# Pooled attention and a gated MLP on one core: 23 of 35 output DMAs move from SyncE's queue to ScalarE's

## The chip, the cores and the metric

The kernel runs on one core of a Trainium2 chip. The metric is the time of one execution on the device in microseconds (us), taken as the median of repeated runs. The core has five engines that run side by side, each with an instruction stream of its own: TensorE (PE in the profile; PEld is its weight loads), VectorE (DVE), ScalarE (ACT), GpSimd (POOL) and SyncE (SP). In this kernel SP computes nothing; it issues DMAs, one after the other. ACT computes and can issue DMAs too. An engine's stream is strictly in order: an instruction that waits holds all that stand behind it on that engine.

## The reference, cut to what matters

```python
# q, k, v: (8, 8, 576, 64), pooled attention
k_p = k.reshape(B, H, Sp, 8, D).mean(axis=3)
v_p = v.reshape(B, H, Sp, 8, D).mean(axis=3)
attn = softmax(q @ k_p.T / sqrt(D))
x = (attn @ v_p).transpose(0, 2, 1, 3).reshape(4608, 512)
# w1, w2: (512, 1024), w3: (1024, 1024), w_out: (1024, 512)
h = ((x @ w1) * (x @ w2)) @ w3
out = h @ w_out                      # (4608, 512) float32
```

## The kernel before, in words

The 4608 tokens are worked on in twelve chunks of 384 (`m` or `n`, 0 to 11); a chunk has three output tiles of 128 tokens (`t`, 0 to 2). fp32 matrices are kept as a high and a low part, and a product is made of three matmul passes (`PASSES`, line 771). At the start `w3 @ w_out` is multiplied once into `W` (`w_mm`, line 1046), so that a chunk needs `a = x @ w1`, `b = x @ w2`, the product `g = a * b`, and `g @ W`.

For chunks 0 to 7 the steps are `a_mm` and `b_mm` (the matmuls of line 783), `a_post` (ACT copies `a` out of PSUM, line 793), `b_post` (DVE multiplies, line 803), `g_hi` (ACT, line 808), `g_lo` (DVE, line 813) and `out_mm` (line 831), eight times (`j`). Chunks 8 to 11 go in two pairs (`M` = 4, 5) with seven products of blocks in place of eight (`prod`, line 960). The blocks of their weights were mixed earlier and written to DRAM (`ws`); SP loads them into a ring of 11 slots, some steps ahead (`load_u`, line 945), each load waiting until PE has read the slot's former block. `s1_copy`, `s5_copy` and `s2_copy` (ACT, lines 966, 971, 974) take the products out of PSUM.

Attention of chunk n+1 runs between these: `s_mm` (line 531), softmax on DVE and ACT (lines 547 to 592), a transposition by way of DRAM: `te_turn` (DVE, lines 656, 657), `te_out` (SP writes `D<-T` and `D<-Tr`, lines 665, 666), `te_in` (SP reads back `PTl<-D` and `PTr<-D`, four DMAs each, lines 687, 691), `te_post` and `te_rest` (ACT, lines 701 and 696; DVE, 703 and 697), then `av_mm` (line 735).

When the matmuls of a chunk's output are done, `out_post` (line 851) copies each of the three PSUM banks to an SBUF tile `ob` (pool `osp`, three buffers, shared with the tiles of the weight mixing) and sends it to DRAM. ACT copies tiles 0 and 2 (line 863), DVE tile 1 (line 861). Chunk 11's tile 2 is split in halves (lines 853 to 858) whose DMAs go out on ACT and SP already (line 857).

The order of each engine's stream is fixed by a hand-made plan of due times (`plan`, `SHIFT`, `LATER`); the change touches none of it. The framework counts the landing of DMAs on eight counters (DMAHW0 to DMAHW7), which the program's DMAs use in turn, whichever engine issues them. A DMA is issued only when the one that used its counter before has landed. So a DMA on one queue can wait for one of the other queue.

Of the kernel before, what the change touches and what calls it, by code (L numbers as in the profile page):

```python
# [19 lines left out]
def kernel(  # L20
# [14 lines left out]
    nc = tc.nc  # L35
# [3 lines left out]
    P = 128  # L39
# [70 lines left out]
        out=msk,  # L110
        in_=ident.rearrange("p (q j e) -> p j q e", j=4, e=KR),
# [707 lines left out]
    def out_t(m, j, t):  # L819
        if j == 0 and t == 0:  # L820
            oacc[m] = [pacc.tile([P, 512], F32, tag=f"o{t}", name=f"o{t}") for t in range(3)]
            if m == NCH - 1:
                oacc["end"] = oacc[m][2], patt.tile([P, 512], F32, tag="att", name="att")
        g, gh, gl = gt[m, j]
        c = slice(t * P, (t + 1) * P)
        parts = [(oacc[m][t], slice(0, DM))]
        if m == NCH - 1 and t == 2:
            parts = [(oacc["end"][i][:, :HD], slice(i * HD, (i + 1) * HD)) for i in range(2)]
        for o, d in parts:
            for i, (sg, sw) in enumerate(PASSES):  # L830
                nc.tensor.matmul(out=o, lhsT=(gh, gl)[sg][:, c], rhs=W[j][sw][:, d],  # L831
                                 start=(j == 0 and i == 0), stop=(j == NJ - 1 and i == 2))
        if t == 2:
            gt.pop((m, j))
        if m == NCH - 1 and j == NJ - 1:
            out_post(m, t)
# [14 lines left out]
    def out_post(m, t):  # L851
        r0 = m * CH + t * P
        if m == NCH - 1 and t == 2:
            for i, copy in enumerate((nc.scalar.copy, nc.vector.tensor_copy)):
                half = p2.tile([P, HD], F32, tag="a", name="a")
                copy(out=half, in_=oacc["end"][i][:, :HD])
                (nc.scalar, nc.sync)[i].dma_start(out=out[r0:r0 + P, i * HD:(i + 1) * HD], in_=half)
            return
        ob = osp.tile([P, DM], F32, tag="ob", name="ob")
        if t == 1:  # L860
            nc.vector.tensor_copy(out=ob, in_=oacc[m][t])  # L861
        else:
            nc.scalar.copy(out=ob, in_=oacc[m][t])
        nc.sync.dma_start(out=out[r0:r0 + P], in_=ob)

    B11, B21, B22, T1, T2, T3, T4 = range(NU)
    HALVES = (0, 2)
# [493 lines left out]
    for m in range(NP):  # L1361
        m0 = M0 + 3 * NJ * m
        for j in range(NJ):
            k = m0 + 3 * j
            at("M", k, a_mm, m, j)
            at("P", k + 1, a_post, m, j)
            at("M", k + 1, b_mm, m, j)
            at("P", k + 2, b_post, m, j)
            at("P", k + 2, g_hi, m, j)
            at("P", k + 2.5, g_lo, m, j)  # L1370
            at("M", k + 5 + 1.2 * ((m, j) == (NP - 1, NJ - 1)), out_mm, m, j)
        for t in range(3):
            at("P", m0 + 3 * NJ + 3 + 2 * (m == NP - 1), out_post, m, t)
# [16 lines left out]
    for M in range(NP // 2, NCH // 2):  # L1390
        m0 = M0 + 6 * NJ * M
        for j in range(NJ):
            k = m0 + STEP * j
            for i, x in enumerate((0, 0.68, 1.24, 1.92, 2.48, 3.16, 4.45)):
                at("M", k + x, prod, M, j, i)
                units.append((int(k + x), M, j, i))
            for fn, x in STEADY.items():
                if fn in (g_hi, g_lo):
                    at("P", k + x, fn, 2 * M, j)
                else:  # L1400
                    at("P", k + x, fn, M, j)
            if j < NJ - 1:
                for x, lo, hi in ((6.8, 0, 1), (8.03, 1, 2), (8.71, 2, 8), (10.56, 8, 9)):
                    at("M", k + x, out_some, 2 * M, j, lo, hi)
            else:
                at("M", k + 5.2, out_some, 2 * M, j, 0, 9)
        k = m0 + STEP * NJ
        for t in range(3):
            at("P", k + 1, out_post, 2 * M, t)
        for j in range(NJ):  # L1410
            at("P", k + j, g1_hi, M, j)
            at("P", k + j, g_lo, 2 * M + 1, j)
            at("M", k + 1 + j + 3.2 * (j == NJ - 1 and M < NCH // 2 - 1), out_mm, 2 * M + 1, j)
        if M < NCH // 2 - 1:
            for t in range(3):
                at("P", k + 5 + NJ, out_post, 2 * M + 1, t)
# [72 lines left out]
```

## Time and profile before

| what | us |
|---|---|
| median of 3 runs | 744.12 (744.02 to 744.53) |
| the profiled execution, its own time | 740.84 |
| span of its instructions | 739.1 |
| PE busy | 731.1 (99%) |
| DVE busy | 461.3 (62%) |
| ACT busy | 351.8 (48%) |
| POOL busy | 175.4 (24%) |

The profile is of one execution. Its own time is 1.7 us above its span and 3.3 us below the median of the runs. Busy is the time in which an engine executes; DMA issues and waits are not counted in it. PE's granted clock is 0.999 of full speed over the span. The first chunk's outputs are copied at 142 us, the last chunk's at 734 us.

### The profile page before, as it was taken

To read this page: it belongs to the slowest core of one execution; us is meant where nothing else is said; L and a number is where in the kernel's file an instruction comes from. 1 tells how busy PE (TensorE), PEld (TensorE's weight loads), DVE (VectorE), ACT (ScalarE), POOL (GpSimd) and SP (SyncE) were. 2 spreads that over 40 slices of the span, in tenths; PEclk is the share of its full clock that TensorE was granted. 3 is DMA by queue.
4 is the path that set the end of the run, shared out by engine and by line. 5 is a ranking of instruction groups with operands and counts; after the bars stand their busy time and mean duration, and the time that the engine had idled before them with its cause. 6 is when DMAs were issued, how large, how long until landed. Compare 5 with 4: busy or idle time off the path is not lost.

```text
span 739.1 us, 12234 instructions
## 1 busy us (share of the span) xinstructions
PE 731.1 (99%) x4088; PEld 682.5 (92%) x4088; DVE 461.3 (62%) x913; ACT 351.8 (48%) x1059; POOL 175.4 (24%) x228
## 2 busy tenths in 40 slices
PE   8999999999999999999999999999999999999997
PEld 7888999999999999999999999999999999899996
DVE  5788877655675835664657658465886586633342
ACT  7888986442442644434433435353454344422222
POOL 2245384033431531004503313044042000000000
PEclk9999999999999999999999999999999999999999
DMA  9979934187386465486656462736498859176611
GB/s 327 344 241 298 330 120 122 55 229 184 109 210 156 145 163 151 128 193 189 176 130 186 130 171 81 148 127 154 96 333 266 226 170 314 41 236 199 197 57 44
DMA packets 177743, 132.62 MB, mean 179 GB/s; under 512 B 78352, under 2 KB 145104, under 8 KB 177680
## 3 DMA queue, kind: packets, MB, share of 16 engines
q1 hardware_dynamic: 177536, 131.70, 62.6%
q8 instruction: 33, 0.54, 0.3%
q14 instruction: 30, 0.25, 0.1%
q10 hardware_dynamic: 144, 0.13, 0.1%
HBM read 94.63 MB, written 37.16 MB: 178 GB/s over the span
## 4 chain that ended last, share of the span: by engine, by line
PE 95%; DMA 2%; DVE 1%; SPq 1%; issue 0%; ACT 0%; ACTq 0%
PE o L831 22%; PE a L783 18%; PE b L783 18%; PE a L960 8%; PE att L531 5%; PE att L735 5%; PE o L1052 4%; PE o L846 4%; PE att L960 4%; PE b L960 2%; DMA raw<-in_moe_w_dram 1%; PE b L1052 1%; PE a L1052 1%; DMA D<-T 1%; PE att L238 1%; DMA PTl<-D 0%
## 5 line engine op out<-in xcount | busy, mean ns | idle before, releaser
L831 PE MATMUL o<-Wc,gh 128*128 128x512 f32 (+1 forms) x480 | 149.2, 392 | 0.0
L783 PE MATMUL b<-xT,hl 128*128 128x384 f32 x768 | 145.7, 339 | 0.0
L783 PE MATMUL a<-xT,hl 128*128 128x384 f32 x768 | 145.6, 338 | 0.0
L783 PEld LDWEIGHTS a<-xT,hl 128*128 128x128 f32 x768 | 133.4, 188 | 2.9
L783 PEld LDWEIGHTS b<-xT,hl 128*128 128x128 f32 x768 | 132.8, 188 | 0.0
L808 ACT CAST gh<-a 128x384 fp32r<-128x384 f32 x80 | 41.1, 514 | 126.8 <-DVE a L803 101.7
L831 PEld LDWEIGHTS o<-Wc,gh 128*128 128x128 f32 x480 | 87.5, 188 | 13.8 <-DVE ob L861 0.2
L831 PE MATMUL o<-Wc,gl 128*128 128x512 f32 (+1 forms) x240 | 93.1, 388 | 0.0
L569 ACT ACTIVATE E<-att,mx 128x72 f32<-128x72 f32 (+1 forms) x240 | 73.3, 323 | 28.3 <-DVE mx L547 26.5
L960 PE MATMUL a<-X,ring 128*128 128x384 f32 x384 | 77.4, 337 | 0.9 <-ACT tmp L974 0.6
L960 PEld LDWEIGHTS a<-X,ring 128*128 128x128 f32 x384 | 67.8, 188 | 4.4 <-ACT tmp L974 1.0
L803 DVE TENSOR_TENSOR a<-b,a 128x384 f32<-128x384 f32 x64 | 35.2, 550 | 55.5 <-PE b L783 53.8
L468 POOL TENSOR_TENSOR st<-st 128x512 f32<-128x512 f32 (+2 forms) x29 | 39.8, 1371 | 114.0 <-DMA st<-in_v_dram 65.2
L793 ACT COPY a<-a 128x384 f32<-128x384 f32 x64 | 30.7, 480 | 75.2 <-PE a L783 75.0
L831 PEld LDWEIGHTS o<-Wc,gl 128*128 128x128 f32 x240 | 45.1, 188 | 10.2 <-DVE gl L813 0.7
L813 DVE TENSOR_TENSOR gl<-a,gh 128x384 fp32r<-128x384 f32 x80 | 47.1, 589 | 7.0 <-ACT gh L808 6.6
L880 POOL TENSOR_TENSOR mix<-mix 128x256 f32<-128x256 f32 x16 | 11.9, 744 | 162.1 <-DMA mix<-wr 118.8
L569 ACT ACTIVATION_READ_ACCUMULATOR E<-att,mx 128x1 f32 (+1 forms) x240 | 50.0, 208 | 0.0
L531 PE MATMUL att<-kbd,qT 128*128 128x144 f32 (+1 forms) x320 | 49.9, 286 | 0.0
L531 PEld LDWEIGHTS att<-kbd,qT 128*128 128x128 f32 (+1 forms) x320 | 45.8, 179 | 1.7
L547 DVE TENSOR_REDUCE mx<-att 128x4 f32<-128x288 f32 (+1 forms) x80 | 35.3, 446 | 15.3 <-PE att L531 14.9
L960 PE MATMUL att<-X,ring 128*128 128x384 f32 x192 | 38.8, 338 | 0.0
(160 smaller groups left out, 1161.9 us busy)
## 6 DMA issues: line engine op xcount, KB each, us to landing
ring<-ws SPq DMA_DIRECT2D x112, 256.0 KB
raw<-in_moe_w_dram SPq DMA_DIRECT2D x32, 512.0 KB
out_dram<-ob SPq DMA_DIRECT2D x35, 256.0 KB
st<-in_v_dram SPq DMA_DIRECT2D x16, 512.0 KB
ws<-mix SPq DMA_DIRECT2D x32, 256.0 KB
st<-in_k_dram SPq DMA_DIRECT2D x24, 288.0 KB
qs<-in_q_dram SPq DMA_DIRECT2D x112, 48.0 KB
D<-T SPq DMA_DIRECT2D x7, 768.0 KB
```

The costliest lines, as they stand in the source:

```text
L468: eng.tensor_tensor(out=t[:, :, 0:4], in0=t[:, :, 0:4], in1=t[:, :, 4:8], op=ALU.add)
L531: nc.tensor.matmul(out=ps[:nt, 2 * KP * j:2 * KP * (j + 1)], lhsT=qT[n][:, pr, off:off + nt], rhs=kbd[b % 2][:, pr], start=True, stop=True,)
L547: nc.vector.tensor_reduce(out=mx[:nt, hs], in_=sv, axis=AX.X, op=ALU.min)
L569: nc.scalar.activation(out=E[:nt, h], in_=sv[:, i], func=AF.Exp, scale=-1.0, bias=mx[:nt, h:h + 1], accum_out=sm[:nt, h:h + 1])
L735: nc.tensor.matmul(out=Tp[n, pr, "x"][:, off:off + cnt], lhsT=parts[x][0], rhs=parts[x][1], start=x == 0, stop=x == 3)
L783: nc.tensor.matmul(out=o, lhsT=w12[j, w][sw][:, kt * P:(kt + 1) * P], rhs=x[sx][:, kt], start=(i == 0), stop=(i == 3 * NK - 1))
L803: nc.vector.tensor_tensor(out=g, in0=ps[:, :CH], in1=g, op=ALU.mult)
L808: nc.scalar.copy(out=gh, in_=g)
L813: eng.tensor_tensor(out=gl, in0=g, in1=f(gh), op=ALU.subtract)
L831: nc.tensor.matmul(out=o, lhsT=(gh, gl)[sg][:, c], rhs=W[j][sw][:, d], start=(j == 0 and i == 0), stop=(j == NJ - 1 and i == 2))
L960: nc.tensor.matmul(out=o, lhsT=w[:, kt, sw], rhs=x[sx][:, kt], start=first and n == 0, stop=n == 5, skip_group_check=True)
L1052: nc.tensor.matmul(out=wacc[h][it], lhsT=w3t[s][sa][:, it * P:(it + 1) * P], rhs=wo[j][sb], start=(j == 0 and i == 0), stop=(j == NJ - 1 a ...
```

## The change

In `out_post` the DMA of a tile that DVE copied (`t == 1`) stays with SP, and the DMA of a tile that ACT copied (tiles 0 and 2 of chunks 0 to 10, tile 0 of chunk 11: 23 of them) is put in ACT's own stream, right behind the copy.

```diff
             nc.vector.tensor_copy(out=ob, in_=oacc[m][t])
         else:
             nc.scalar.copy(out=ob, in_=oacc[m][t])
-        nc.sync.dma_start(out=out[r0:r0 + P], in_=ob)
+        (nc.sync if t == 1 else nc.scalar).dma_start(out=out[r0:r0 + P], in_=ob)
```

The streams of PE, DVE and POOL are the same as before. Three places show what moves. `waits` names the counters that an instruction waits for: those of DMA landings, and those of the engines.

ACT at the outputs of chunk 7 (`ob_6272` and `ob_6278` are tiles 0 and 2), before:

```order
L569 ACTIVATE E_6190,sm_6192<-att_6179,mx_6191 96x72 x3
L863 COPY ob_6272<-o0_5599 128x512 [waits PE_49]
L863 COPY ob_6278<-o2_5601 128x512 [waits PE_49]
L966 COPY a_6305<-a_6296 128x384 [waits PE_49,Activation_49]
L569 ACTIVATE E_6282,sm_6284<-att_6267,mx_6283 96x72 [waits DVE_49,Activation_49]
```

and now:

```order
L863 COPY ob_6272<-o0_5599 128x512 [waits PE_49]
L864 DMA out_0_dram<-ob_6272 128x512 [waits DMAHW7_49,Activation_49]
L863 COPY ob_6278<-o2_5601 128x512 [waits PE_49]
L864 DMA out_0_dram<-ob_6278 128x512 [waits DMAHW2_49,Activation_49]
L966 COPY a_6305<-a_6296 128x384 [waits PE_49]
```

Each DMA waits for ACT's own copy and for a landing, and stands ahead of the next copy and of line 966.

SP at the same place, before:

```order
L945 DMA ring_6270<-ws_102 128x512 [waits DMAHW0_49,PE_49]
L864 DMA out_0_dram<-ob_6272 128x512 [waits DMAHW1_49,Activation_49]
L864 DMA out_0_dram<-ob_6275 128x512 [waits DMAHW2_49,DVE_49]
L864 DMA out_0_dram<-ob_6278 128x512 [waits DMAHW3_49,Activation_49]
L945 DMA ring_6303<-ws_102 128x512 [waits DMAHW4_49,PE_49]
L945 DMA ring_6331<-ws_102 128x512 [waits DMAHW5_49,PE_49]
L945 DMA ring_6333<-ws_102 128x512 [waits DMAHW6_49,PE_49]
L665 DMA D_6335<-T_6251 96x1024 [waits DMAHW7_49,DVE_49]
```

and now:

```order
L864 DMA out_0_dram<-ob_6275 128x512 [waits DMAHW3_49,DVE_49]
L945 DMA ring_6303<-ws_102 128x512 [waits DMAHW4_49,PE_49]
L945 DMA ring_6331<-ws_102 128x512 [waits DMAHW5_49,PE_49]
L945 DMA ring_6333<-ws_102 128x512 [waits DMAHW6_49,PE_49]
L665 DMA D_6335<-T_6251 96x1024 [waits DMAHW7_49,DVE_49]
```

SP has one output there in place of three and waits for DVE's copy alone. The transposition's write of line 665 now shares counter 7 with ACT's output `ob_6272`.

SP at the outputs of chunk 5, the four `PTr` reads (line 691) of the transposition, before:

```order
L691 DMA PTr_4706<-D_4842 32x3x128 [waits DMAHW5_49]
L691 DMA PTr_4706<-D_4842 32x3x128 [waits DMAHW6_49]
L691 DMA PTr_4706<-D_4842 32x3x128 [waits DMAHW7_49]
L691 DMA PTr_4706<-D_4842 32x3x128 [waits DMAHW0_49]
L358 DMA qs_4859<-in_q_dram 32x12x32 [waits DMAHW1_49]
```

and now:

```order
L691 DMA PTr_4706<-D_4842 32x3x128 [waits DMAHW7_49]
L691 DMA PTr_4706<-D_4842 32x3x128 [waits DMAHW0_49]
L691 DMA PTr_4706<-D_4842 32x3x128 [waits DMAHW1_49]
L691 DMA PTr_4706<-D_4842 32x3x128 [waits DMAHW2_49]
L358 DMA qs_4859<-in_q_dram 32x12x32 [waits DMAHW3_49]
```

The counters of ACT's two outputs of chunk 5 are 7 and 1: the first of the four reads now waits until tile 0 has landed, the third until tile 2 has.

## Rows read from the trace of the kernel before

**Rows 1.** The page's part 1: busy time, share of the span, instructions.

```profile
PE 731.1 (99%) x4088; PEld 682.5 (92%) x4088; DVE 461.3 (62%) x913; ACT 351.8 (48%) x1059; POOL 175.4 (24%) x228
```

**Rows 2.** Waits of PE's matmuls: who waited for whom, total us, times, longest.

```profile
...
PE a L960 <- ACT tmp L974: 0.6, 1, 0.6
PE a L960 <- DVE tmp L985: 0.3, 1, 0.3
```

**Rows 3.** Waits of SP's queue, the longest row.

```profile
SPq L864 <- ACT ob L863: 66.5, 9, 22.2
```

**Rows 4.** DMA issues by line: times, ns min/median/max, first and last start.

```profile
L864 SPq DMA_DIRECT2D out_dram<-ob x35: 332/371/565, 143.5 to 735.3; - x35
L945 SPq DMA_DIRECT2D ring<-ws x112: 319/326/1767, 521.2 to 700.6; - x112
```

**Rows 5.** Timeline of chunk 11's outputs: start, us, engine, line, what.

```profile
734.51 1.13 SPq L864 DMA_DIRECT2D out_dram<-ob  x2
735.30 0.42 DVE L856 COPY a<-att 128x256 f32<-128x256 f32 x1
735.35 0.37 ACTq L857 DMA_DIRECT2D out_dram<-a  x1
735.75 0.38 SPq L857 DMA_DIRECT2D out_dram<-a  x1
```

**Rows 6.** Timeline of chunk 7's outputs, on DVE, ACT, SP, PEld.

```profile
546.82 0.65 DVE L861 COPY ob<-o 128x512 f32<-128x512 f32 x1
...
547.85 1.07 ACT L863 COPY ob<-o 128x512 f32<-128x512 f32 x2
...
548.46 1.31 SPq L864 DMA_DIRECT2D out_dram<-ob  x3
...
549.86 1.50 SPq L945 DMA_DIRECT2D ring<-ws  x3
550.01 0.48 ACT L966 COPY a<-a 128x384 f32<-128x384 f32 x1 [1.09 <-PE a L960]
...
552.10 1.00 PEld L960 LDWEIGHTS att<-X,ring 128*128 128x128 f32 x6 [0.20 <-ACT tmp L971]
```

**Rows 7.** Timeline of chunk 2's outputs: ACT behind them, and PE.

```profile
259.59 0.48 ACT L793 COPY a<-a 128x384 f32<-128x384 f32 x1
...
262.69 1.03 PE L783 MATMUL a<-xT,hl 128*128 128x384 f32 x5
```

**Rows 8.** Timeline behind chunk 10's last output: ACT, DVE, PEld.

```profile
718.67 0.52 ACT L999 CAST gh<-g 128x384 fp32r<-128x384 f32 x1
...
719.22 0.56 DVE L813 TENSOR_TENSOR gl<-g,gh 128x384 fp32r<-128x384 f32 x1 [0.64 <-ACT gh L999]
...
720.64 0.19 PEld L831 LDWEIGHTS o<-Wc,gl 128*128 128x128 f32 x1
```

**Rows 9.** Timeline of chunk 5's outputs, on ACT, SP, PE.

```profile
425.94 0.59 ACT L863 COPY ob<-o 128x512 f32<-128x512 f32 x1 [0.39 <-PE o L831]
426.47 1.84 SPq L691 DMA_DIRECT2D PTr<-D  x4
...
431.93 0.82 ACT L696 CAST PTr<-PTr 64x768 fp32r<-64x768 f32 x1
...
434.35 0.27 PE L735 MATMUL att<-PTr,VR 128*128 128x192 f32 x1
```

**Rows 10.** SP's timeline of chunk 0's outputs; line 874 reuses tile 0's buffer.

```profile
143.55 1.33 SPq L864 DMA_DIRECT2D out_dram<-ob  x3
...
145.65 0.63 SPq L874 DMA_DIRECT2D mix<-wr  x1
```

**Rows 11.** The chain of work that ended last, behind chunk 7's outputs.

```profile
560.55 1.05 PE att L960 x6
562.48 5.38 DMA D<-T
...
569.19 3.52 DMA PTl<-D
```

## The prediction

> **What bounds the kernel now.** I read the page first, then PE's waits, then SP's, then the timelines around the places where outputs leave. PE is busy for 731.1 of a span of 739.1 us [rows 1], so all of its idle time is 8.0 us. Of that some 3.8 lie behind its last matmul: DVE's last copy starts at 735.30, right behind PE's end, and the span ends at 739.1 [rows 5]. PE's waits have six rows: four belong to the weights' preparation (lines 236 to 264), ahead of any output, and the two that are shown come later, of 0.6 and 0.3 us, both around the start of the block products [rows 2]. So between the first output and the last matmul there is 0.9 us that a better order of transfers could give back, and the reader should see from this that a large gain is not there to be had, however long SP's waits are. SP does wait long for the copies that ACT makes: 66.5 us in nine waits, the longest of 22.2 [rows 3]. None of it shows up on PE: what SP loads is loaded early.
>
> **The change, part by part.** *On ACT, 23 issues are added.* ACT's one issue in this trace, for chunk 11's half tile, took 0.37 us [rows 5], and SP's 35 issues of outputs 0.33 to 0.57, median 0.37 [rows 4]. The issue also breaks the overlap of neighbouring copies (two of 0.59 take 1.07 together, so 0.1 is lost) and needs a gap of about 0.1 to the next instruction (three of SP's issues take 1.31, against 1.11 for three medians) [rows 4, 6]. That makes 0.57 us of ACT's stream for each output, 13 us in all, on an engine that is busy for 352 of 739 us [rows 1]. Whether it costs time is decided at each of the twelve places:
>
> - Chunks 0, 2, 6: the two copies run back to back, so what follows on ACT comes 2 x 0.57 = 1.14 us later. Chunk 2 is the tightest: line 793's copy of `a` moves from 259.59 to 260.73 and ends at 261.21, and PE writes that bank again at 262.69 [rows 7]. Slack 1.5 us, cost nothing. Were both issues as slow as SP's slowest of all, 1.77 [rows 4], 2.8 more would be asked and 1.3 lost.
> - Chunk 7: the copies start at 547.85; 1.07 + 1.14 later it is 550.06, and line 966, which waits for PE, started at 550.01 [rows 6]. So 0.05 us late. Here nothing is spare: two copies later PE's weight load already waits 0.20 us for ACT [rows 6], so a delay goes through to PE one to one. With issues of 0.33 it is nothing, with 0.57 it is 0.45. I take 0.05, since the median is what ACT's own issue showed.
> - Chunks 1, 3, 4, 5, 8, 9, 10, 11: the second copy waits for PE anyhow, and ACT idles behind it. Chunk 10 is the tightest: line 999's cast moves from 718.67 to 719.24, line 813 from 719.22 to 719.79, done at 720.35, and PE loads that tile at 720.64 [rows 8]. Cost nothing.
>
> *Do ACT's issues wait for landings?* Each also waits for the DMA that used its counter before. I followed all 23 through the order: the former user is a DMA that SP issued at least 4 us earlier in this trace. No wait is forecast.
>
> *On SP, 23 issues and their waits go.* What stays is tile 1, which waits for DVE's copy. At chunk 7 that copy ends at 547.47, where ACT's first ends at 548.44 and SP issued at 548.46 [rows 6]. One issue of 0.4 behind 547.5, SP is at its ring loads at 547.9, which it reached at 549.86 [rows 6]: up to 1.9 us earlier. Does PE gain? The late wait of 0.6 [rows 2] hangs on a chain that I followed backwards: a product's copy on ACT stands behind the casts of the transposition, those behind `PTl<-D` (3.52 us), that behind `D<-T` (5.38 us), issued at 562.48, behind ring loads, one of which waits for PE's matmuls that end at 561.60 (560.55 + 1.05): there the chain passes from PE to SP [rows 11]. Its start is set by PE, not by what SP did at 548. But 5.38 us is long for such a transfer because ring loads are under way beside it, and with some of them done earlier it can land sooner. Gain between nothing and the 0.6 of the wait; I take 0.3.
>
> The Trainium skill, "DMA: Bandwidth & Descriptors", "Issuing engines are not separate DMA queues", has it that issuing from several engines saves only sequencer time, since the same 16 DMA engines do the work. By that alone the 0.3 would be nothing; no run here has shown it yet.
>
> *New waits on SP.* SP now waits for landings of ACT's outputs at chunks 3, 4, 5 and 7. The tightest is chunk 5: tile 2 can be issued at 426.57 (its copy starts at 425.94 and takes 0.59), and the third `PTr` read, issued near 427.39 (two of four in 1.84 us), must wait for its landing [rows 9]. The one landing that the trace shows is chunk 0's: issued at 143.55, its buffer written again at 145.65, 2.1 us [rows 10]. So the read goes at 428.67, 1.28 late, and the fourth at about 429.1. With 2.1 us to land it is there by 431.2, and ACT needs it at 431.93 [rows 9]; with the 3.52 of rows 11 it is there at 432.6, 0.7 late, of which PE, which uses the result at 434.35, would see some 0.4. I take 0.2. The far end: an output that takes 5.38 to land, followed by a read of 3.52, brings ACT's cast to 436 and costs about 4.
>
> *The tail.* Chunk 11's tile 0 leaves ACT before the half tile's copy, and the last DMA is still SP's at 735.75, behind DVE's copy that ends at 735.72 [rows 5]. Nothing.
>
> The sum is +0.05 - 0.3 + 0.2, about zero: 740.8 us for an execution like the profiled one (740.84; span 739.1 and 1.7 around it). It lies 3.3 us below the median of the runs shown, which I put on again: **744.1 us**.
>
> **The rivals.**
>
> *ACT is held at chunk 7 (slower).* If an issue on ACT takes as long as SP's slowest, 1.77 against 0.37 [rows 4], the two cost 2.8 us more; PE waits for all of it: 746.9. It decides from 1.5 us on, so when the pair takes 2.2 us and not 0.74. For it: SP's issues do stretch now and then where DMAs are dense, and they are dense there. Against: none of the 35 outputs took over 0.57 [rows 4].
>
> *ACT's issue stands while SP issues (no measurable change, by way of a small loss).* At chunk 7 SP issues ring loads just when ACT issues. If ACT has to stand for one of SP's issues each time, 2 x 0.37 = 0.74 us go to PE: 744.9. Against it: in the tail SP's second output (735.3 to 735.6) and ACT's issue (735.35 to 735.72) lie over each other, and ACT's took 0.37, as if alone [rows 5]. The Trainium skill, "Perfetto Trace Analysis", "DMA Instruction — HWDGE (DVE, Sync)", says that the block that generates descriptors is shared and locked by one sequencer at a time, which speaks against this change; that one overlap of the trace doesn't agree.
>
> *SP's wait at chunk 5 reaches PE (slower).* The far end above: 748. It needs an output to take over 3.5 us to land, which the one landing shown, 2.1, speaks against.
>
> *SP's freedom pays (faster).* Both late waits of PE vanish, 0.9 us [rows 2]: 743.2. To pass the bound of a measurement, the 3.8 of the tail would have to shrink too, or the runs without a profile, 3.3 us longer, would have to hold waits on transfers that the profiled one doesn't.
>
> **How the numbers follow.** A measurement of this kernel can tell about 0.2%, 1.5 us, from no change. The forecast, with all of its small terms, has 0.68; the standing issue, also within the bound, 0.09; so "same" has 0.77. The held ACT has 0.10 and SP's wait 0.05: "slower" 0.15. "Faster" has 0.08, mostly for what the profiled execution can't show. The range goes from 742.9 (both waits of PE gone, and 0.3 for the scatter of the runs) to 746.0 (the standing issue and 1.1 of the two slow cases); about 2 in 10 lie outside.
>
> **What would show it.** Right: PE's waits stay six or seven small rows, ACT's new issues take 0.33 to 0.6 each, line 966 starts within 0.1 us of PE's matmul, SP's first row, 66.5 us for ACT's copies, is gone, and ring loads behind chunk 7 start up to 2 us earlier against PE's work. Wrong: a row in which PE waits over 1 us for ACT behind line 864; an ACT issue over 1 us; a wait of ACT for `PTr<-D` near chunk 5; or a shorter tail.

## The result, and the profile after

The changed kernel takes 747.73 us (median of 6 runs, 746.77 to 749.19) against 744.07 us for the kernel before on the same chip (6 runs, 741.09 to 745.25): ratio 1.0059, 95% interval 1.0037 to 1.0081. (The ratios are worked out from the single runs; the quotient of the two medians is 1.0049.) In a second set on another occasion, with more runs, it was 745.62 (10 runs) against 742.07 (31 runs): 1.0044, interval 1.0031 to 1.0057. So it is some 3.5 us slower; both intervals lie above 1. The forecast was no change, 744.1 us within 742.9 to 746.0. In runs 1 and 10 below, one execution each took over 1200 us at a granted clock of 0.56, and the medians given there leave it out.

The first profiled execution is the slowest of its six, 749.19 us, with a span of 747.3; where a number matters I give it from a second one too, of 746.27 us and a span of 744.4. The page's part 1 of the first, to be laid beside [rows 1]:

```profile
PE 733.5 (98%) x4088; PEld 683.8 (92%) x4088; DVE 458.4 (61%) x913; ACT 353.2 (47%) x1059; POOL 174.9 (23%) x228
```

The engines do the same work. PE's busy time is 2.4 us longer; its idle time went from 8.0 us to 13.8. Who PE's matmuls wait for (the view of [rows 2]: who waited for whom, total us, times, longest):

```profile
PE a L960 <- ACT tmp L974: 2.3, 1, 2.3
...
PE att L531 <- DVE E L551: 1.2, 1, 1.2
PE o L831 <- DVE gl L813: 1.2, 1, 1.2
...
PE att L531 <- DVE xT L768: 0.6, 1, 0.6
PE att L735 <- DVE PTl L703: 0.6, 1, 0.6
```

The last four are new: PE now waits for DVE in the attention and in the products of the first half, where it had waited for nothing. SP's queue shows why (the view of [rows 3], cut to the outputs):

```profile
SPq L864 <- DVE ob L861: 72.1, 6, 21.4
...
SPq L874 <- DMA out_dram<-ob: 6.8, 2, 4.3
SPq L691 <- DMA out_dram<-ob: 6.2, 3, 3.9
...
SPq L358 <- DMA out_dram<-ob: 3.4, 2, 2.8
SPq L665 <- DMA out_dram<-ob: 3.2, 1, 3.2
```

The 66.5 us that SP stood for ACT's copies [rows 3] are gone, but 72.1 us for DVE's copy of tile 1 took their place; no wait of PE is put down to them. Below them stand waits for the landing of an output. Those in front of `PTr` reads, q loads and a `D<-T` write (and one of 4.2 us in front of a ring load) are new; in front of the loads for the weight mixing (line 874) the kernel before had them too:

```profile
SPq L874 <- DMA out_dram<-ob: 2.8, 4, 1.1
```

Line 874 may overwrite the buffer that an output left from (the pool is shared); the others neither read nor overwrite an output, and all that they have in common with it is the counter.

Where the time went, by stretches (from:to, us, PE busy (instructions), granted clock, DMA share, GB/s). The kernel before has 20.00 in the first three and the last of these stretches and 0.59 us of idle time in the fourth. First execution of the changed kernel:

```profile
320.00:340.00 20.00, 18.23 (x101) 1.00 0.81 188
380.00:400.00 20.00, 18.65 (x108) 1.00 0.47 109
440.00:460.00 20.00, 19.39 (x121) 1.00 0.50 129
560.00:580.00 20.00, 18.65 (x104) 1.00 0.85 247
580.00:600.00 20.00, 19.07 (x110) 0.91 0.82 223
```

and the second:

```profile
320.00:340.00 20.00, 18.79 (x103) 1.00 0.86 209
380.00:400.00 20.00, 18.32 (x106) 1.00 0.54 122
440.00:460.00 20.00, 19.28 (x121) 1.00 0.48 127
560.00:580.00 20.00, 18.70 (x103) 1.00 0.81 244
580.00:600.00 20.00, 20.00 (x124) 1.00 0.83 229
```

The first three are chunks 3, 4 and 5: 1.77 + 1.35 + 0.61 = 3.7 us in one execution, 1.21 + 1.68 + 0.72 = 3.6 in the other. That is as much as the medians differ by, and in runs 2, 3 and 7, where SP issues the outputs of these chunks, PE is busy for 20.00 us in all three stretches. The stretch around chunk 7 adds 0.7 in both, and the last one differs between them; but that part is no sign of the change. From 540 to 600 us PE's idle time is 0.9 us in the kernel before, 2.1 in run 3, where SP issues all outputs as before, and 1.1 in run 11, where ACT issues those of chunk 7.

**Chunk 3, step by step.** SP's queue before (start, us, what), in four of its rows:

```profile
312.50 2.68 SPq L691 DMA_DIRECT2D PTr<-D  x4
315.81 0.31 SPq L390 DMA_DIRECT2D st<-in_k_dram  x1
316.67 2.09 SPq L864 DMA_DIRECT2D out_dram<-ob  x3
...
321.99 0.54 SPq L874 DMA_DIRECT2D mix<-wr  x1
```

and now:

```profile
313.21 7.57 SPq L691 DMA_DIRECT2D PTr<-D  x4
320.82 0.40 SPq L390 DMA_DIRECT2D st<-in_k_dram  x1
321.32 0.36 SPq L864 DMA_DIRECT2D out_dram<-ob  x1
```

The four reads take 7.57 us from first to last instead of 2.68, and the load of k behind them leaves 5.0 us later (0.7 of it was there before, at the first of the four). Before, SP issued the outputs *behind* these loads; now ACT's output takes its counter ahead of them. For 3.9 us SP stands in front of the third read for that output. The shift of the counters does one thing more: the landing of an earlier k load, which held the fourth read for 1.0 us, now holds the second, for 2.2 us (1.6 in the second execution). The chain of work that ended last goes through it (start, us, what):

```profile
313.29 6.69 DMA out_dram<-ob
...
320.82 4.36 DMA st<-in_k_dram
...
326.59 0.56 DVE gl L813
...
327.19 0.96 PE o L831 x3
```

The output takes 6.69 us to land, the k load 4.36; DVE starts on the k tile (line 468) at 325.20 instead of 322.25, in order, and the tile `gl` that PE needs stands behind it on DVE. PE waits 1.21 us.

The k load ends last in this chain, but the larger part of DVE's delay was there before it, from the `PTr` reads. Line 696 on ACT reads the half of the tile that the first two reads fill, line 697 on DVE the half of the third and fourth:

```profile
320.97 0.84 ACT L696 CAST PTr<-PTr 64x768 fp32r<-64x768 f32 x1 [0.97 <-DMA PTr<-D]
...
322.65 0.95 DVE L697 TENSOR_TENSOR PTr<-PTr 64x768 fp32r<-64x768 f32 x1 [1.66 <-ACT PTh L701]
...
325.20 0.69 DVE L468 TENSOR_TENSOR st<-st 72x512 f32<-72x512 f32 x1 [0.54 <-DMA st<-in_k_dram]
```

DVE stands 1.66 us in front of line 697. The view names line 701, whose tile line 697 doesn't read; in the second execution it puts the same wait, 1.64 us, down to `PTr<-D`. For the k tile DVE stands only 0.54 us more (0.27 in the second). Line 703, behind line 697 on DVE, is also what PE's wait of 0.56 us in line 735 is for. Run 5 has the `PTr` part alone:

```profile
322.12 0.95 DVE L697 TENSOR_TENSOR PTr<-PTr 64x768 fp32r<-64x768 f32 x1 [1.43 <-ACT PTh L701]
...
324.05 0.68 DVE L468 TENSOR_TENSOR st<-st 72x512 f32<-72x512 f32 x1
```

There DVE doesn't wait for k at all, and PE still waits 0.59 us for `gl`. So what hurts at chunk 3 is the fourth `PTr` read first, and the k load behind it second.

At chunk 4 the held transfers are q loads. SP has 32 of them to issue there, the last 24 of them between 382.47 and 394.91 with little else between; the last eight start at 390.91 where they started at 385.41, 5.5 us later, of which 2.5 had been lost before chunk 4 (0.7 ahead of chunk 3, 1.8 in it):

```profile
390.91 4.00 SPq L358 DMA_DIRECT2D qs<-in_q_dram  x8
```

DVE waits for them up to 2.53 us at a time (line 373), the softmax comes late, and PE's scores (line 531) wait 1.2. At chunk 5 it is the same by way of line 691 (3.26 us for the landing, in the chain) and the twelve q loads behind it.

On ACT all is as forecast. Issues by line (times, ns min/median/max), and chunk 7 on ACT, to be laid beside [rows 6]:

```profile
L864 ACTq DMA_DIRECT2D out_dram<-ob x23: 338/338/376, 144.3 to 742.7; - x23
```

```profile
553.24 0.59 ACT L863 COPY ob<-o 128x512 f32<-128x512 f32 x1
553.86 0.34 ACTq L864 DMA_DIRECT2D out_dram<-ob  x1
554.24 0.59 ACT L863 COPY ob<-o 128x512 f32<-128x512 f32 x1 [0.41 <-ACT ob L863]
554.86 0.34 ACTq L864 DMA_DIRECT2D out_dram<-ob  x1
555.34 0.48 ACT L966 COPY a<-a 128x384 f32<-128x384 f32 x1 [0.51 <-PE a L960]
```

Line 966 starts at 555.34, 0.04 us behind the end of the PE product that it reads (of its 0.51 us of idle time 0.34 is the issue): the two issues cost nothing at the place where I had counted each tenth.

### The profile page after: what moved, and what is told of

It reads as the page before. It is cut to its first block, busy times and chain, and to the rows that moved or that the text cites. A ratio compares the mean times of both kernels' runs of the same rounds, so it can differ in the third digit from the quotient of the medians.

```text
span 747.3 us, 12205 instructions
## 1 busy us (share of the span) xinstructions
PE 733.5 (98%) x4088; PEld 683.8 (92%) x4088; DVE 458.4 (61%) x913; ACT 353.2 (47%) x1059; POOL 174.9 (23%) x228
## 4 chain that ended last, share of the span: by engine, by line
PE 86%; DMA 6%; DVE 4%; SPq 2%; ACT 1%; issue 1%; ACTq 0%; DVEq 0%
PE o L831 19%; PE a L783 15%; PE b L783 15%; PE a L960 8%; PE att L531 5%; PE att L735 4%; PE o L1052 4%; PE o L846 4%; PE att L960 4%; PE b L960 2%; DMA out_dram<-ob 1%; DMA D<-T 1%; SPq L358 1%; DMA raw<-in_moe_w_dram 1%; PE b L1052 1%
## 5 line engine op out<-in xcount | busy, mean ns | idle before, releaser
L831 PEld LDWEIGHTS o<-Wc,gh 128*128 128x128 f32 x480 | 87.5, 188 | 13.8 <-DVE ob L861 0.2
```

## The experiments

All ratios are against the kernel before, run beside each on the same chip; intervals are 95%.

**1. Only the four places where SP's new waits matter**

```diff
-        (nc.sync if t == 1 else nc.scalar).dma_start(out=out[r0:r0 + P], in_=ob)
+        (nc.scalar if t != 1 and m in (3, 4, 5, 7) else nc.sync).dma_start(out=out[r0:r0 + P], in_=ob)
```

> Chunks 3, 4, 5 and 7 alone: ScalarE issues their eight outputs, SyncE the other fifteen. Theory (SyncE stands in its queue for landings of ScalarE's outputs, at L691 and L390 of chunk 3, L358 of chunk 4, L691 of chunk 5, L665 and L945 of chunk 7, and the work behind these reaches PE): the counters of these places are those of the changed kernel, so nearly all of its loss stays, 746.8 to 748.2 against 744.1 before, ratio 1.004 to 1.006, and PE's idle time between 320 and 340 us is over 1 us again. Rival A (ScalarE loses its issue time, 0.34 us each, or its copies come later): 8 of 23 issues, a third of the loss, 745.3. Rival B (the transfers from ScalarE's ring collide with others, whoever waits): also a third, 745.3.

746.53 us (5 runs) against 742.09, ratio 1.0065 (1.0047 to 1.0084). The whole loss is there with 8 of the 23 issues. The profile of this kernel is read in run 11.

**2. The complement**

```diff
+        (nc.sync if t == 1 or m in (3, 4, 5, 7) else nc.scalar).dma_start(out=out[r0:r0 + P], in_=ob)
```

> The complement: ScalarE issues the fifteen outputs of chunks 0, 1, 2, 6 and 8 to 11, SyncE those of 3, 4, 5 and 7. Theory: no wait of SyncE for a ScalarE output that is still under way is left on a path to PE, so 743.6 to 744.6, ratio 0.9995 to 1.0007. Rivals A and B: 15 of 23 issues, two thirds of the loss, 746.5.

743.08 us, ratio 1.0014 (1.0002 to 1.0026): a little over the expected end of 1.0007, and far from 746.5. PE is busy for 20.00 of 20 us in each of the stretches of chunks 3, 4 and 5, although SP still waits for ACT's outputs, in front of a load for the weight mixing and a ring load (who waited for whom, us, times, longest):

```profile
SPq L874 <- DMA out_dram<-ob: 7.2, 4, 4.1
SPq L945 <- DMA out_dram<-ob: 4.2, 1, 4.2
```

These two rows are as long as those of the changed kernel and cost next to nothing: what stands behind them in the queue is not needed soon.

**3. ACT's time alone**

```diff
             nc.scalar.copy(out=ob, in_=oacc[m][t])
+            nc.scalar.copy(out=ob[:, :P], in_=oacc[m][t][:, :P])
```

(on the kernel before, with all outputs issued by SP)

> The kernel before with a second ScalarE copy of the tile's first 128 columns behind each of the 23 copies (the same values again), all outputs issued by SyncE: ScalarE loses about 0.3 us at each of the places where the change made it issue, and no queue changes. Theory: nothing, 743.8 to 744.7 (ratio 0.9997 to 1.0008). Rival A (ScalarE's time): the whole loss, 746.8 to 748.2.

743.43 us, ratio 1.0010 (0.9997 to 1.0022). ACT is busy for 357.5 us instead of 351.8, and nothing of these 5.7 us comes through that a measurement can tell. (The 23 issues of 0.34 us would be 7.8, so three quarters of their time is put back here.) ACT's time is not the cause.

**4. The 23 outputs issued by GpSimd**

```diff
+        (nc.sync if t == 1 else nc.gpsimd).dma_start(out=out[r0:r0 + P], in_=ob)
```

> The same 23 outputs issued by GpSimd, whose transfers count their landings on counters of their own, so that nothing of SyncE waits for an output of another engine. Theory: SyncE is as free as in the changed kernel and has no new wait; what is left is GpSimd standing for ScalarE's copies in front of its splits of k and its weight sums: 743.6 to 745.2. SyncE's L691 at chunk 3 takes under 3.5 us for four where it took 7.57. Rival A: ScalarE issues nothing, 744.1. Rival B (outputs that leave at once collide with the loads): the whole loss, 747.

745.85 us, ratio 1.0046 (1.0030 to 1.0061). A miss: no wait of SP for an output is left at chunks 3 to 5, and PE's idle time there is down to 0.6 us, but the kernel is slow again. A part of the loss is now in the tail. GpSimd's last issue and SP's last:

```profile
738.91 0.54 POOL L864 DMA_DIRECT2D out_dram<-ob  x1 [15.13 <-ACT ob L863]
...
739.88 0.40 SPq L857 DMA_DIRECT2D out_dram<-a  x1
```

The span ends at 745.6, which is 5.3 us behind the end of SP's last issue at 740.28; before it is 3.0 (735.75 + 0.38 to 739.1) [rows 5]. That would be 2.3 of the 3.4 us that the ratio stands for, from one execution; that GpSimd's last output lands late there is read from this distance alone. What this run does give is the time of an output from issue to landing, which the trace of the other queues doesn't state (min/median/max):

```profile
DMA to landing us min/median/max: 2.3/3.9/6.6
```

**5 to 7. One place at a time**

```diff
+        (nc.scalar if t != 1 and m == 3 else nc.sync).dma_start(out=out[r0:r0 + P], in_=ob)
...
+        (nc.scalar if t != 1 and m in (4, 5) else nc.sync).dma_start(out=out[r0:r0 + P], in_=ob)
...
+        (nc.scalar if t != 1 and m == 7 else nc.sync).dma_start(out=out[r0:r0 + P], in_=ob)
```

> Chunk 3's two outputs alone are issued by ScalarE. Theory: SyncE's third L691 and the k load L390 behind it wait for their landings (four L691 take about 7.5 us from first to last, against 2.68 before), PE has its idle time of 1 to 2 us between 320 and 340 us and nowhere else anew; time 1.8 us over the kernel before, 1.2 to 2.4, ratio 1.0016 to 1.0032. Rivals (ScalarE's time, collisions): two of 23 issues, 0.3 us, ratio 1.0004.

743.64 us, ratio 1.0008 (0.9994 to 1.0023): under the expected 1.0016, and by the time alone not to be told from the rivals' 1.0004. But the mechanism is in its profile, at half the size: SP's four line 691 take 7.05 us, and PE waits 0.6 for `gl` in the stretch from 320 to 340 and nowhere else anew.

> Chunks 4 and 5 alone: four outputs issued by ScalarE. Theory: PE idle 1.35 us between 380 and 400 (q loads L358 late) and 0.6 us between 440 and 460, 2.0 us in all over the kernel before, 1.3 to 2.6, ratio 1.0018 to 1.0035. Rivals: four of 23 issues, 0.7 us, ratio 1.0009.

744.32 us, ratio 1.0027 (1.0011 to 1.0043), as the theory had it; PE idles 1.17 us between 380 and 400 and 0.66 between 440 and 460.

> Chunk 7 alone: two outputs issued by ScalarE. Theory: SyncE's L665 (D<-T) waits for the first output's landing, PE's wait for tmp (L974) is over 2 us instead of 0.6, time 1.0 to 2.5 us over the kernel before (1.7 of idle time, less if the fall of the granted clock behind it in the changed kernel's profile belongs to that one execution), ratio 1.0013 to 1.0034. Rivals: 0.3 us, ratio 1.0004.

742.63 us, ratio 0.9999 (0.9985 to 1.0014). A miss: SP does wait 2.6 us for ACT's output in front of the `D<-T` write, and PE's wait for `tmp` is 0.8 us, as before within 0.2. By itself chunk 7 costs nothing.

**8. The same eight transfers without a shared counter**

```diff
+        (nc.gpsimd if t != 1 and m in (3, 4, 5, 7) else nc.sync).dma_start(out=out[r0:r0 + P], in_=ob)
```

> Chunks 3, 4, 5 and 7 alone, their eight outputs issued by GpSimd (landings on counters of its own), all others by SyncE, so the same eight transfers leave early as in the run with ScalarE at these four chunks, and the tail is that of before. Theory: no wait of SyncE for them, 0 to 1 us over the kernel before (0.4 us of idle time was left between 320 and 340 us and 0.5 us between 540 and 560 us with all 23 on GpSimd), ratio 1.000 to 1.0014. Rival B (the early transfers themselves hurt): ratio 1.0065 as with ScalarE.

743.49 us, ratio 1.0007 (0.9992 to 1.0021). The six outputs of chunks 3, 4 and 5 are issued 0.3 us behind the end of their copies, where ACT issued them 0.03 behind (those of chunk 7 are 2.2 us behind and more), the tail is that of before, and 1.0065 has become 1.0007. The landings are as slow as those of ACT's outputs:

```profile
DMA to landing us min/median/max: 2.8/5.4/6.4
```

But SP waits for none of them. SP's queue at chunk 3:

```profile
312.49 2.18 SPq L691 DMA_DIRECT2D PTr<-D  x4
315.36 0.31 SPq L390 DMA_DIRECT2D st<-in_k_dram  x1
```

2.18 us for the four reads where ACT's outputs made it 7. So it isn't the early transfers that hurt, and not their collision with the loads, but SP's standing for them.

**9 to 12. Do the places add up?** By the ratios, the single places give 0.6 + 2.0 + 0 = 2.6 us, and all four together gave 4.8.

```diff
+        (nc.scalar if t != 1 and m in (3, 4, 5) else nc.sync).dma_start(out=out[r0:r0 + P], in_=ob)
...
+        (nc.scalar if t != 1 and m in (4, 5, 7) else nc.sync).dma_start(out=out[r0:r0 + P], in_=ob)
```

> Chunks 3, 4 and 5 issued by ScalarE, 7 by SyncE. The single places gave 0.6 (chunk 3), 2.0 (chunks 4 and 5) and 0 us (chunk 7), 2.6 together, where all four at once gave 4.8. Theory A (the surplus of 2 us arises around chunk 7, where ScalarE's outputs hold L665 once PE and the DMAs come there with another phase): 2.6 us over the kernel before, ratio 1.0035. Theory B (it arises from chunks 3, 4 and 5 together, chunk 7's issue adds nothing): 4.5 us, ratio 1.006.

745.77 us, ratio 1.0046 (1.0031 to 1.0061): theory A's 1.0035 and B's 1.006 both lie within the interval.

> Chunks 4, 5 and 7 issued by ScalarE, 3 by SyncE. Theory A (surplus around chunk 7, called forth by any earlier loss): 2.0 of chunks 4 and 5 and about 2 around chunk 7, ratio 1.005, with PE's wait for tmp (L974) over 2 us. Theory B (the surplus needs chunk 3): 2.0 us, ratio 1.0027.

745.07 us, ratio 1.0043 (1.0027 to 1.0058): again both lie within it, A's 1.005 well inside, B's 1.0027 at its end. PE's wait for `tmp` was 1.7 us.

> The same kernel as the first run with chunks 3, 4, 5 and 7 on ScalarE, for a profile at full clock: ratio 1.005 to 1.008 again; PE idle over 0.6 us in 320 to 340, about 1.2 in 380 to 400 and 0.6 in 440 to 460; where the remaining 1 to 3 us stand is what is asked (theory A: between 540 and 600 us).

745.87 us, ratio 1.0053 (1.0034 to 1.0073). Idle time of PE in its profile: 1.22, 1.17 and 0.61 us at chunks 3, 4 and 5, together 3.0; around chunk 7 it is 1.07 (0.30 and 0.77), next to 0.93 before, so nothing.

> The changed kernel again, beside the others on the same chip: ratio 1.004 to 1.008. Its second profile says what of the idle time is there in each execution: 380 to 400 (1.35) and 440 to 460 (0.6) within 0.3 us of the first, 320 to 340 between 0.6 and 1.8, and the fall of the granted clock behind PE's wait at L960 between 580 and 600 only if that wait is about 2 us again.

The changed kernel itself, 1.0044, shown above.

The four runs don't tell the two theories of the surplus apart, and the profiles make a surplus doubtful altogether: chunk 3 costs 0.6 to 1.8 us from one execution to the next (0.64, 1.13, 1.21, 1.22 and 1.77 in the five that have it on ACT), chunks 4 and 5 together 1.3 to 2.4 (1.30, 1.35, 1.78, 1.83, 1.96 and 2.40 in six), and every measured sum carries an interval of a us or more to either side. 3 to 5 us is what the places make together. The profiles give chunk 7 no share in it: from 540 to 600 us PE idles 0.9 to 2.4 us in the six with SP's outputs at chunk 7, and 1.1 to 2.6 in the five with ACT's. Whether it adds something now and then stays open.

## Why the prediction was wrong

**The step that failed** is the term "New waits on SP", for which I took 0.2 us, where the runs show 3 to 5. It had the mechanism: SP would wait for landings of ACT's outputs at chunks 3, 4, 5 and 7. Three things in it were wrong.

- *The landing.* I took 2.1 us, from the one buffer that was written again [rows 10], and called 3.52 and 5.38 the bounds. The runs showed 6.69 and 3.26 us at chunks 3 and 5, and 2.3 to 6.6 with a median of 3.9 for 23 outputs sent by GpSimd. 2.1 lies below all of them. It was not "the one landing that the trace shows" either: SP waits four times for one in front of line 874, and at chunk 3 the wait ends at 321.99, where the three outputs had been issued from 316.67 to 318.43. That is 5.3 us for the first, whose buffer line 874 would take as at chunk 0, and at least 3.6. The DMA engines' load tells the cases apart: their share was 0.54 between 143 and 146 us, where the 2.1 was read, 1.05 between 316.7 and 322.0, and in the changed kernel 1.04 between 313.3 and 320.0, where the output took 6.69.
- *The place.* I worked out chunk 5 as "the tightest", by when ACT needs the read that is held. But the third and fourth reads, which are held, are needed by DVE's line 697 and not by ACT's line 696, and it was at chunk 3 that they came late for it. The rest of the cost stood behind the held transfer in SP's queue, which I did not follow: the k load at chunk 3, the q loads at chunks 4 and 5.
- *The slack.* All of it rested on the sentence "None of it shows up on PE: what SP loads is loaded early", drawn from long waits of SP that cost PE nothing. Those waits stand where the queue has time; at chunk 4 SP issues q loads back to back, 16 of them in 7.72 us, and the delay of its queue, 3.0 us beyond what PE had lost, was still there at the last of them. An average of waits says nothing about one stretch.

So the far end of that term, "about 4" and 748, with a chance of 0.05, was the outcome, though by another path than the one described: not through `PTr` and ACT at chunk 5, but through `PTr`, the k load and DVE at chunk 3 and through q loads at chunks 4 and 5, in the second execution 1.2, 1.7 and 0.7 us. That the size agrees is chance.

**Point by point, the rest.**

- The ceiling of a gain, 0.9 us of PE's late waits: it held, and nothing of it was gained.
- ACT's 23 issues at 0.37 us, and 0.05 us of cost: right, 0.338 in the median, and nothing on PE (run 3).
- No wait of ACT's issues for a landing: right, all 23 start 0.02 or 0.03 us behind the end of their copies. The view puts 0.49 us ahead of a copy at chunk 5 down to a q load and 2.53 ahead of line 966 at 661.09 down to an output; but 0.34 of the first is ACT's own issue, and the PE product that line 966 reads ends at 661.05.
- SP freed at chunk 7, gain of 0.3: not seen. The ring loads came earlier, but the `D<-T` write behind them was held for 3.2 us by ACT's output (2.0 in the second execution), and PE's wait on that chain was 2.3 and 1.3 us instead of 0.6. That isn't shown to be the change's doing: it was 1.3 and 1.6 in runs 2 and 3, where SP issues chunk 7's outputs.
- By the rule of the Trainium skill, "DMA: Bandwidth & Descriptors", "Issuing engines are not separate DMA queues", that only sequencer time is saved, the 0.3 would have been nothing. The trace agrees with that, and the runs add a loss that this rule doesn't give: run 8 against run 1.
- The tail: right, SP's last issue at 743.94 and the span's end at 747.3 lie as far apart as before [rows 5].
- ACT held at chunk 7 and ACT's issue standing while SP issues: both refuted by the one row, 338/338/376. The lock that the Trainium skill describes in "Perfetto Trace Analysis", "DMA Instruction — HWDGE (DVE, Sync)", shows no price here.

The sign of being wrong that I named was half right: I had a wait of ACT for `PTr<-D` near chunk 5. It came at chunk 3, 0.97 us in line 696, for a read that SP had held for a k load. The waits that cost time were DVE's, for `PTr`, k and q.

## What to carry to other kernels

When a DMA moves to another engine, list for each of the old queue's DMAs whose landing it now waits for, and cost that wait at whoever needs the held transfer and at what stands *behind* it in the queue, in the stretches where the queue issues without a pause; a queue that stands for 66.5 us of the span without harm can still be the limit of one stretch. Take the landing time from a stretch with the same DMA load, not from the one place that shows it. Here a transfer that shares its counter with urgent loads was better issued behind them on their own queue than early on another.

## What the runs showed that was not expected

- *Landing time and load.* The same 256 KB output lands in about 2.1 us at a DMA share of 0.54, in 3.26 at 0.74, and in 6.69 at 1.04 (the stretches 143 to 146, 431.2 to 434.5 and 313.3 to 320.0 us; the view's share can pass 1). Run 8, where GpSimd issues, has two more at each place: 2.8 and 3.1 us at chunk 5 (0.81), 5.5 and 5.7 at chunk 4 (1.08), 6.3 and 6.4 at chunk 3 (1.09). They are few, but they are the size of the error.
- *PE's clock behind a wait.* In the first execution of the changed kernel PE waited 2.28 us until 580.93, and the granted clock fell to the lower level for some 3 us (columns as above, stretches of 2 us):

```profile
576.00:578.00 2.00, 2.00 (x13) 1.00 0.84 223
578.00:580.00 2.00, 0.65 (x4) 1.00 0.43 103
580.00:582.00 2.00, 1.07 (x3) 0.71 0.82 190
582.00:584.00 2.00, 2.00 (x7) 0.50 0.84 230
```

0.50 is 1.2 of 2.4 GHz. Six products of line 960 took 2.29 us there and 1.31 in the kernel before behind its shorter wait, and the six of line 846 behind them 1.92 against 1.37: 1.5 us more, given to a wait of 2.3. It fell likewise behind the wait of 1.9 us in run 6, and not behind those of 1.3 (the second execution) and 1.7 (run 10). That may be part of why single executions of these kernels scatter by 3 us.
